# Capped attention and two expert layers on one core: a q load on another queue, a v copy on another engine, a 64-column transpose and a last tile copied in two halves

## The chip, the core and the metric

The program runs on one core of one Trainium2 chip. The metric is the device time of one execution in microseconds (us), the median of several runs. The engines named below are PE (TensorE, matrix products), DVE (VectorE), ACT (ScalarE), POOL (GpSimd) and SP (SyncE, which only issues transfers here). Each engine takes its instructions in order; ACT and SP also issue DMA transfers, in order with the rest of their work.

## The reference, cut to what matters

```python
scores = q @ k^T / sqrt(64)               # 2 batches x 12 heads, 448 x 64 each
scores = cap * tanh(scores / cap)         # cap = 30
attn = exp(scores - max);  attn /= sum(attn)
x = (attn @ v), heads side by side        # 896 tokens x 768
h = x @ w_in1;   g = elu(h);     x = g @ w_out1     # 768 -> 2048 -> 768
h = x @ w_in2;   g = relu(h)**2; out = g @ w_out2   # the same sizes
```

Inputs and output are float32 in HBM; the four weight matrices arrive as float64 words.

## The kernel before, in words

**Precision.** Every float32 operand x of a product is split into a high part (rounded to the PE's float32r format) and a low part (x minus the high part). A product of two operands is three PE products: high by high, high by low, low by high. So each operand costs a copy (the high part) and a subtraction (the low part) on some engine.

**Attention.** The 24 heads are worked on in 12 pairs (`n` from 0 to 11); two pairs make a group `g` whose k, q and v come with the same loads. A head has 448 rows: three full blocks of 128 and a last one of 64. `load_group` (L103) issues the loads. `what` says which: "k" loads three blocks of k and its last rows (into `kz`, where the rest is zero, two transfers, L127), "q" loads three blocks of q (L118) and its last 64 rows (into `qz`, L122), "v" three blocks of v (L133), "w" its last rows (`vs`, L139). All go out on SP's queue except the first pair's q, the cap and the first weights, which go out on ACT's.

For each pair, `turn` (L170) has the PE transpose four blocks of k and four of q into the tile `pt` in PSUM (L168; there is one such tile), `high` (L186, ACT) and `low` (L192, DVE) split them. `scores` (L235, PE) makes a fourth of the scores into one of two `sc` tiles, `tanh` (L244, ACT) and `exp` (L252, ACT) follow, `split_p` (L263 copy, L264 subtraction, both DVE) splits the result into `ph` and `pl`, and `pv` (L287, PE) multiplies by v, whose parts `vh` and `vl` were made by `prep_v` (L153 copy on POOL for pairs 0 and 1 and on DVE from pair 2 on; L154 subtraction on POOL). `pv_out` (L296, ACT) copies the sums out; `norm` and `norm_x` (L309, L327 to L334, DVE, with three small transfers on SP's queue) divide by the row sums and split the result into `xh` and `xl`. The order of the work in the loop L574 is written by hand and overlaps four pairs: while pair n is at its tanh, pair n-1 is at its second half of `pv`, pair n+1 at its `high` and `low`, pair n+2 at its transposes. In iteration n the DVE's order is: second half of `split_p(n-1)`, `prep_v(n+1)`, `low(n+1)`, then `norm(n-2)`, `norm_x(n-3)`, first half of `split_p(n)`. In iterations 1 and 2 the DVE also makes one piece of weights (`second`, L607, L587).

Before the loop, `first_pair` (L198) turns and splits pair 0 in three pieces, with products of the identity matrix in between (L196, `idle_products`) whose results nobody reads. Its copies (L220, ACT) and subtractions (L222, DVE) are of 384, 512 and 128 columns. After it come the scores of pair 0 and `turn(1)`; `turn(2)` is issued in iteration 0 (L612), ahead of `pv(0, 0)`.

The issue order of the loads at the start, on SP's queue (L537 to L547): pair 0's k; pair 1's k and q; pair 0's v; the second group's k and q (L544); pair 1's v; weights; the second group's v.

**Expert layers.** The weights stream in by pieces, are turned from float64 words into high and low parts on DVE and ACT, and four stages of products follow (L521 to L523, then L745 to L747 for the last). The last stage writes the output by blocks of 128 tokens and 432, then 336 columns: `evac_out` (L730) copies one PSUM accumulator to a tile `o`, on DVE for even token blocks and on ACT for odd ones (L732), and SP issues the store (L733). The last of these is token block 6, alone in its group (L758).

The lines that set this order:

```python
load_group(1, "kq")                                        # L544
(nc.vector if n > 1 else nc.gpsimd).tensor_copy(h, vn)     # L153, in prep_v(n)
nc.tensor.transpose(to, src, ident)                        # L168, in turn_one
(nc.scalar.copy if t % 2 else nc.vector.tensor_copy)(o, acc)   # L732
```

Of the kernel before, what the change touches and what calls it, by code (L numbers as in the profile page):

```python
# [26 lines left out]
def attention_moe_kernel(  # L27
# [12 lines left out]
    nc = tc.nc  # L40
    B, H, S, D = q.shape
    NT, DM = out.shape
    DFF = w_in1.shape[1]
    P = 128
    NFULL = S // P
# [10 lines left out]
    ident = const.tile([P, P], F32, name="ident")  # L56
# [24 lines left out]
    W = 512  # L81
# [18 lines left out]
        if i < 2:  # L100
            eng.memset(vss[i][:, :, D:], 1.0)

    def load_group(g, what="kqvw", pp=None, dma=nc.sync.dma_start):  # L103

        if 2 * g >= len(pairs):
            return
        b, hp = pairs[2 * g]
        h0, nh = (0, 4) if pp is None else (2 * pp, 2)
        hs = slice(2 * hp + h0, 2 * hp + h0 + nh)
        if g not in nat:  # L110
            nat[g] = {x: lp.tile([P, NFULL, 4, D], F32, name=x, tag=x) for x in "kqv"}
        tail = slice(NFULL * P, S)
        for x, src in (("k", k), ("q", q)):
            if x in what:
                t = nat[g][x][:, :, h0:h0 + nh]
                src = src[b, hs]
                for c in range(NFULL):
                    dma(  # L118
                        t[:, c], src[:, c * P:(c + 1) * P].rearrange("h p d -> p h d")
                    )  # L120
                if x == "q":
                    dma(  # L122
                        qzs[g % 2][:D, h0:h0 + nh], src[:, tail].rearrange("h p d -> p h d")
                    )
                else:
                    for hh, r in enumerate(ROWS):
                        dma(  # L127
                            kzs[g % 2][r, h0 // 2:(h0 + nh) // 2, r],
                            src[hh::2, tail].rearrange("h p d -> p h d"),
                        )  # L130
        if "v" in what:
            for c in range(NFULL):
                dma(  # L133
                    nat[g]["v"][:, c, h0:h0 + nh],
                    v[b, hs, c * P:(c + 1) * P].rearrange("h p d -> p h d"),
                )
        if "w" in what:
            for hh, r in enumerate(ROWS):
                dma(  # L139
                    vss[g % 2][r, h0 // 2:(h0 + nh) // 2, :D],  # L140
                    v[b, hs][hh::2, tail].rearrange("h p d -> p h d"),
                )

    def prep_v(n):
        if n >= len(pairs):
            return
        g, pp = divmod(n, 2)
        vh, vl = vhs[n % 3], vls[n % 3]
        vn = nat[g]["v"][:, :, 2 * pp:2 * pp + 2]
        h, l = (t.rearrange("p (c h) d -> p c h d", h=2)[:, :, :, :D] for t in (vh, vl))  # L150


        (nc.vector if n > 1 else nc.gpsimd).tensor_copy(h, vn)  # L153
        nc.gpsimd.tensor_tensor(l, vn, h.bitcast(F32), op=ALU.subtract)  # L154


# [2 lines left out]
    def turn_one(to, n, u, c):  # L159
        g, pp = divmod(n, 2)  # L160
        hs = slice(2 * pp, 2 * pp + 2)
        if c < NFULL:
            src = nat[g]["kq"[u]][:, c, hs].rearrange("p h d -> p (h d)")
        elif u == 0:
            src = kzs[g % 2][:, pp]
        else:
            src = qzs[g % 2][:, hs].rearrange("p h d -> p (h d)")
        nc.tensor.transpose(to, src, ident)  # L168

    def turn(n):  # L170
        if n >= len(pairs):
# [26 lines left out]
    def first_pair():  # L198

        idle = psc.tile([P, 2, W], F32, name="sc", tag="sc")
        warm = lambda n: idle_products(idle, n)
        qk = [ap_.tile([P, 2, W], F32R, name=x, tag=x) for x in ("kqh", "kql")]
        st["qk", 0] = qk
        warm(8)
        pieces = []
        for u, cs, pool, tag, after in (
            (0, range(NFULL), ps1, "pt", 2),
            (1, range(NFULL + 1), ps1, "po", 0),  # L210
            (0, range(NFULL, NFULL + 1), psc, "sc", 6),
        ):
            t = pool.tile([P, 2, W], F32, name=tag, tag=tag)
            at = slice(cs[0] * P, (cs[-1] + 1) * P)
            for c in cs:
                turn_one(t[:, u, c * P:(c + 1) * P], 0, u, c)
            warm(after)
            pieces.append((t[:, u, at], *(x[:, u, at] for x in qk)))
        for t, h, l in pieces:
            nc.scalar.copy(h, t)  # L220
        for t, h, l in pieces:
            nc.vector.tensor_tensor(l, t, h.bitcast(F32), op=ALU.subtract)  # L222
# [115 lines left out]
    N0, N1 = 432, 336  # L338
# [196 lines left out]
    with tc.manual_schedule():  # L535
        fill_kq(0, nc.vector)
        load_group(0, "k", 0)  # L537
        load_group(0, "q", 0, dma=nc.scalar.dma_start)
        nc.scalar.dma_start(capt, cap.unsqueeze(0).to_broadcast([P, 1]))
        ws.load(nc.scalar.dma_start)  # L540
        load_group(0, "kq", 1)
        load_group(0, "vw", 0)
        fill_kq(1, nc.gpsimd)
        load_group(1, "kq")  # L544
        load_group(0, "vw", 1)
        ws.load()
        load_group(1, "vw")  # L547
# [2 lines left out]
        fill_v(2, nc.gpsimd)  # L550
        np_ = len(pairs)
        first_pair()
        nc.vector.reciprocal(tsc, capt)
        nc.vector.tensor_scalar(tsc, tsc, 1.0 / math.sqrt(D), None, op0=ALU.mult)
        prep_v(0)
# [18 lines left out]
        for n in range(np_):  # L574
            last = n == np_ - 1
            tanh(n, 0)
            if n:
                high(n + 1)
            tanh(n, 1)
            if not n:  # L580
                high(n + 1)
            split_p(n - 1, 1)
            prep_v(n + 1)
            exp(n, 0)
            low(n + 1)
            if n == 2:
                emit(second[3:])  # L587
            scores(n, 2)
            pv(n - 1, 1)
            scores(n, 3)  # L590
            if n:
                turn(n + 2)
            else:
                idle_products(ps1.tile([P, 2, W], F32, name="po", tag="po"), 9)
            norm(n - 2)
            if last:
                emit(ws.start())
            tanh(n, 2)
            pv_out(n - 1)
            if 2 <= n < 7:  # L600
                ws.load()
            tanh(n, 3)
            exp(n, 1)
            emit(norm_x(n - 3))
            split_p(n, 0)
            if n == 1:
                second = ws.whole()  # L607
                emit(second[:3])
            scores(n + 1, 0)
            scores(n + 1, 1)  # L610
            if not n:
                turn(2)  # L612
            if last:

                begun.append(new_acc())
                mm_in(0, 0, begun[0], xh, xl, kb[0:6:2])
            pv(n, 0)

            if n % 2:
                load_group((n + 3) // 2, "qv" if n > 1 else "v")  # L620
            else:
                load_group(n // 2 + 2, "k" if n else "kq")
                load_group(n // 2 + 1, "w" if n else "")


# [101 lines left out]
                todo = parts_of(acc[:, :, :S], yh, yl, m)  # L727
            return todo

        def evac_out(t, acc, c0, n):  # L730
            o = ep.tile([P, N0], F32, name="o", tag="e")[:, :n]
            (nc.scalar.copy if t % 2 else nc.vector.tensor_copy)(o, acc)  # L732
            nc.sync.dma_start(out[t * P:(t + 1) * P, c0:c0 + n], o)  # L733

        def moe2_out(todo, gh, gl):
            nt = NT // P

            def banks(n, width):
                tiles = [new_acc() for _ in range((n + 1) // 2)]
                return [tiles[i // 2][:, i % 2, :width] for i in range(n)]  # L740

            def mm(acc, f, t, w):
                gs = slice(t * P, (t + 1) * P)
                a, z = f == 0, f == FC - 1
                nc.tensor.matmul(acc, gh[:, f, gs], w[0], start=a, stop=False)  # L745
                nc.tensor.matmul(acc, gh[:, f, gs], w[1], start=False, stop=False)  # L746
                nc.tensor.matmul(acc, gl[:, f, gs], w[0], start=False, stop=z)  # L747

            acc = banks(nt, N0)
            for f in range(FC):  # L750
                w = ws.get((3, f))
                for t in range(nt):
                    mm(acc[t], f, t, w)
                emit(todo + ws.advance() + ws.advance())
                todo = []
            for t in range(nt):
                evac_out(t, acc[t], 0, N0)
            groups = [[0, 1], [2, 3], [4, 5], [6]]  # L758
            for ts in groups:
                acc = banks(len(ts), N1)  # L760
                for f in range(FC):
                    w = chunk(late["w"], f)
                    for a, t in zip(acc, ts):
                        mm(a, f, t, w)
                for a, t in zip(acc, ts):
                    evac_out(t, a, N0, N1)

        gh = gp.tile([P, FC, NT], F32R, name="gh", tag="gh")
        gl = gp.tile([P, FC, NT], F32R, name="gl", tag="gl")
# [45 lines left out]
```

## Time and profile before

| | us |
|---|---|
| median of 3 runs (595.73 to 596.18) | 595.95 |
| the profiled execution, whole | 594.1 |
| its span, first to last instruction | 592.3 |
| PE busy, of the span | 583.4 (98%) |
| DVE busy | 425.0 (72%) |
| ACT busy | 334.2 (56%) |
| POOL busy | 32.1 (5%) |

The profile is of one execution, taken by the hardware. An engine's rows give start and duration of its instructions and, in square brackets, how long the engine was idle before and what released it. Times inside the span count from its first instruction. "PEclk" is the granted clock of the PE as a share of full speed; rows show 1.00 (2.4 GHz) and 0.50 (1.2 GHz). "DMA share" is the mean busy share of the core's 16 DMA engines. The time between the span and the whole execution is 594.1 - 592.3 = 1.8 us. Durations overlap by a little where an engine begins an instruction before the last one is through.

### The profile page before, as it was taken

The page shows a single profiled execution, that of the slowest core. Times are in us where ns is not written, and L with a number is a line of the kernel's source. Part 1 is how long each engine was busy: PE and PEld are TensorE (multiplying, and loading weights), DVE is VectorE, ACT ScalarE, POOL GpSimd, SP SyncE. Part 2 cuts the span into 40 slices and gives each one's busy share as a digit, 9 for nine tenths or more (in the row PEclk, how much of TensorE's full clock was granted, in tenths as well). Part 3 has the DMA queues.
Part 4 walks back from the last instruction along what each step waited for, and adds up shares of the span by engine and source line. Part 5 has one row for each costly group of instructions (what it writes and reads, how often), then busy time and mean ns, then how long its engine had stood idle before and what let it go on. Part 6 is the DMA issues. An engine that isn't in the chain of part 4 may idle for free.

```text
span 592.3 us, 8596 instructions
## 1 busy us (share of the span) xinstructions
PE 583.4 (98%) x3062; PEld 528.0 (89%) x3062; DVE 425.0 (72%) x845; ACT 334.2 (56%) x484; POOL 32.1 (5%) x46
## 2 busy tenths in 40 slices
PE   8899999999999999999999999999999999999997
PEld 8677777788999999999999999999999999999997
DVE  4599999989999888665666657777777599981000
ACT  5699999827898777433333335666666645441000
POOL 3110110000000000000000000000000011230000
PEclk9899999999999999999999999999999999999999
DMA  5645651024444333233333344333333346622000
GB/s 128 158 103 140 161 148 42 33 75 144 135 133 134 106 98 100 76 128 106 116 98 107 111 132 132 107 107 107 108 114 113 108 136 184 184 70 106 24 23 37
DMA packets 81980, 64.76 MB, mean 109 GB/s; under 512 B 38416, under 2 KB 77072, under 8 KB 81936
## 3 DMA queue, kind: packets, MB, share of 16 engines
q1 hardware_dynamic: 80432, 63.58, 36.8%
q10 hardware_dynamic: 1504, 0.62, 0.4%
q8 instruction: 24, 0.39, 0.3%
q14 instruction: 20, 0.16, 0.1%
HBM read 61.34 MB, written 2.80 MB: 108 GB/s over the span
## 4 chain that ended last, share of the span: by engine, by line
PE 90%; DMA 3%; DVE 3%; SPq 2%; ACT 1%; issue 1%; POOL 0%; ACTq 0%; POOLq 0%; DVEq 0%
PE acc L522 19%; PE acc L523 19%; PE acc L521 19%; PE po L287 8%; PE acc L746 7%; PE acc L745 7%; PE acc L747 7%; PE sc L235 4%; PE pt L168 1%; DMA q<-in_q_dram 1%; SPq L118 1%; DVE xn L327 1%; DMA far<-rd 1%; DMA bc<-far 1%; DMA qz<-in_q_dram 0%
## 5 line engine op out<-in xcount | busy, mean ns | idle before, releaser
L521 PE MATMUL acc<-xh,wh 128*128 128x448 f32 x384 | 139.8, 364 | 1.2 <-ACT xh L333 1.2
L522 PE MATMUL acc<-xl,wh 128*128 128x448 f32 x384 | 140.0, 365 | 0.2 <-DVE xl L334 0.2
L523 PE MATMUL acc<-xh,wl 128*128 128x448 f32 x384 | 139.9, 364 | 0.0
L446 ACT CAST wh<-wf 128x384 fp32r<-128x384 f32 (+2 forms) x114 | 57.9, 508 | 107.2 <-PE acc L522 87.5
L391 ACT ACTIVATE wf<-wst 128x384 f32<-128x384 f32 (+2 forms) x130 | 70.5, 543 | 60.5 <-DVE wl L441 33.7
L441 DVE TENSOR_TENSOR wl<-wf,wh 128x384 fp32r<-128x384 f32 (+2 forms) x116 | 63.6, 548 | 55.9 <-ACT wh L446 55.8
L521 PEld LDWEIGHTS acc<-xh,wh 128*128 128x128 f32 x384 | 72.1, 188 | 7.1 <-ACT xh L333 1.5
L522 PEld LDWEIGHTS acc<-xl,wh 128*128 128x128 f32 x384 | 72.1, 188 | 5.9 <-DVE xl L334 0.5
L523 PEld LDWEIGHTS acc<-xh,wl 128*128 128x128 f32 x384 | 72.1, 188 | 5.7 <-DVE wl L441 0.3
L432 DVE SCALAR_TENSOR_TENSOR wf<-wst,wf 128x384 uint32<-128x384 uint32 (+3 forms) x132 | 71.1, 539 | 0.1
L425 DVE SCALAR_TENSOR_TENSOR wf<-wst,wf 128x384 uint32<-128x384 uint32 (+3 forms) x132 | 70.9, 537 | 0.0
L522 PE MATMUL acc<-gl,wh 128*128 128x448 f32 x192 | 70.0, 365 | 0.0
L523 PE MATMUL acc<-gh,wl 128*128 128x448 f32 x192 | 70.0, 364 | 0.0
L521 PE MATMUL acc<-gh,wh 128*128 128x448 f32 x192 | 69.8, 364 | 0.0
L404 DVE TENSOR_SCALAR wf<-wf 128x384 uint32<-128x384 uint32 (+3 forms) x132 | 54.4, 412 | 0.7
L400 DVE TENSOR_SCALAR wf<-wf 128x384 f32<-128x384 f32 (+3 forms) x132 | 45.7, 346 | 7.5 <-ACT wf L391 7.5
L244 ACT ACTIVATE e<-sc,tsc 128x896 f32<-128x896 f32 (+1 forms) x48 | 43.4, 911 | 2.9 <-PE sc L235 2.9
L732 DVE COPY o<-acc 128x432 f32<-128x432 f32 (+1 forms) x8 | 4.5, 557 | 53.8 <-PE acc L747 45.7
L746 PE MATMUL acc<-wl,gh 128*128 128x432 f32 x112 | 40.3, 359 | 0.0
L745 PE MATMUL acc<-wh,gh 128*128 128x432 f32 x112 | 40.0, 357 | 0.0
L747 PE MATMUL acc<-wh,gl 128*128 128x432 f32 x112 | 39.9, 356 | 0.0
L252 ACT ACTIVATE e<-e,capt 128x1792 f32<-128x1792 f32 (+1 forms) x24 | 38.6, 1609 | 0.8
(94 smaller groups left out, 933.0 us busy)
## 6 DMA issues: line engine op xcount, KB each, us to landing
wst<-in_moe_w_in_dram SPq DMA_DIRECT2D x63, 384.0 KB, 3.2
wst<-in_moe_w_out_dram SPq DMA_DIRECT2D x24, 384.0 KB, 3.2
wst<-in_moe_w_out_dram SPq DMA_DIRECT2D x16, 432.0 KB, 3.2
wst<-in_moe_w_out_dram SPq DMA_DIRECT2D x16, 336.0 KB, 2.9
wst<-in_moe_w_out_dram SPq DMA_DIRECT2D x12, 256.0 KB, 2.7
bc<-far SPq DMA_DIRECT2D x12, 224.0 KB, 3.3
k<-in_k_dram SPq DMA_DIRECT2D x15, 128.0 KB, 3.7
q<-in_q_dram SPq DMA_DIRECT2D x15, 128.0 KB, 2.9
```

What stands on the lines that cost most here:

```text
L391: nc.scalar.activation(self.f[i], hi.bitcast(F32), AF.Abs)
L404: v.tensor_scalar(fb, fb, 3, 0x3FFFFFFF, op0=ALU.logical_shift_left, op1=ALU.bitwise_and)
L425: v.scalar_tensor_tensor(out=fb, in0=hi, scalar=0xC0000000, in1=fb, op0=ALU.bitwise_and, op1=ALU.bitwise_or,)
L432: v.scalar_tensor_tensor(out=fb, in0=lo, scalar=29, in1=fb, op0=ALU.logical_shift_right, op1=ALU.bitwise_or,)
L441: (v if dst is None else nc.gpsimd).tensor_tensor(wl, self.f[i], wh.bitcast(F32), op=ALU.subtract)
L446: (v.tensor_copy if self.alone else nc.scalar.copy)(wh, self.f[i])
L521: nc.tensor.matmul(acc, w[0], x[0], start=first, stop=False)
L522: nc.tensor.matmul(acc, w[0], x[1], start=False, stop=False)
L523: nc.tensor.matmul(acc, w[1], x[0], start=False, stop=last)
L745: nc.tensor.matmul(acc, gh[:, f, gs], w[0], start=a, stop=False)
L746: nc.tensor.matmul(acc, gh[:, f, gs], w[1], start=False, stop=False)
L747: nc.tensor.matmul(acc, gl[:, f, gs], w[0], start=False, stop=z)
```

## The change

Four edits:

1. The second group's q (three transfers of 128 KB) is no longer issued on SP's queue between that group's k and pair 1's v; it is issued on ACT's queue right after `first_pair`. The last rows of q get a letter of their own, "z", and stay on SP's queue.
2. `prep_v(2)` makes its copy on POOL, not on DVE (POOL for n up to 2).
3. The last block of q, which has 64 rows, is transposed at 64 rows and 64 columns, not at 128; in `first_pair` the copy and the subtraction of q cover 448 columns, not 512.
4. The last output tile (token block 6, columns 432 to 767) is copied in two halves of 168 columns: DVE copies the first and SP stores it, ACT copies the second and stores it from its own queue.

```diff
-    def load_group(g, what="kqvw", pp=None, dma=nc.sync.dma_start):
+    def load_group(g, what="kqzvw", pp=None, dma=nc.sync.dma_start):
...
-                if x == "q":
-                    dma(
-                        qzs[g % 2][:D, h0:h0 + nh], src[:, tail].rearrange("h p d -> p h d")
-                    )
-                else:
+                if x == "k":
                     for hh, r in enumerate(ROWS):
                         dma(
                             kzs[g % 2][r, h0 // 2:(h0 + nh) // 2, r],
                             src[hh::2, tail].rearrange("h p d -> p h d"),
                         )
+        if "z" in what:
+            dma(qzs[g % 2][:D, h0:h0 + nh], q[b, hs, tail].rearrange("h p d -> p h d"))
...
-        (nc.vector if n > 1 else nc.gpsimd).tensor_copy(h, vn)
+        (nc.vector if n > 2 else nc.gpsimd).tensor_copy(h, vn)
...
-        nc.tensor.transpose(to, src, ident)
+        if u and c == NFULL:
+            nc.tensor.transpose(to[:, :D], src[:D], ident[:D, :D])
+        else:
+            nc.tensor.transpose(to, src, ident)
...
-            at = slice(cs[0] * P, (cs[-1] + 1) * P)
+            at = slice(cs[0] * P, min((cs[-1] + 1) * P, (W, S)[u]))
...
-        load_group(0, "q", 0, dma=nc.scalar.dma_start)
+        load_group(0, "qz", 0, dma=nc.scalar.dma_start)
...
-        load_group(0, "kq", 1)
+        load_group(0, "kqz", 1)
         load_group(0, "vw", 0)
         fill_kq(1, nc.gpsimd)
-        load_group(1, "kq")
+        load_group(1, "kz")
...
         first_pair()
+        load_group(1, "q", dma=nc.scalar.dma_start)
...
-                load_group((n + 3) // 2, "qv" if n > 1 else "v")
+                load_group((n + 3) // 2, "qzv" if n > 1 else "v")
             else:
-                load_group(n // 2 + 2, "k" if n else "kq")
+                load_group(n // 2 + 2, "k" if n else "kqz")
...
-        def evac_out(t, acc, c0, n):
+        def evac_out(t, acc, c0, n, parts=1):
             o = ep.tile([P, N0], F32, name="o", tag="e")[:, :n]
+            if parts == 2:
+                for i, (copy, dma) in enumerate((
+                    (nc.vector.tensor_copy, nc.sync.dma_start),
+                    (nc.scalar.copy, nc.scalar.dma_start),
+                )):
+                    h = slice(i * n // 2, (i + 1) * n // 2)
+                    copy(o[:, h], acc[:, h])
+                    dma(out[t * P:(t + 1) * P, c0 + h.start:c0 + h.stop], o[:, h])
+                return
...
-                    evac_out(t, a, N0, N1)
+                    evac_out(t, a, N0, N1, 2 if t == nt - 1 else 1)
```

## Rows read from the trace of the kernel before

**Rows 1.** The page, part 1: busy us (share of the span) and instructions.

```profile
PE 583.4 (98%) x3062; PEld 528.0 (89%) x3062; DVE 425.0 (72%) x845; ACT 334.2 (56%) x484; POOL 32.1 (5%) x46
```

**Rows 2.** The chain that ended last, in order of time: start us, us, what.

```profile
17.06 2.67 DMA qz<-in_q_dram
...
20.17 4.06 PE po L287 x12
...
30.18 2.67 PE po L287 x12
...
62.49 0.89 PE pt L168 x8
...
80.91 1.42 PE sc L235 x12
...
89.45 1.42 PE sc L235 x12
...
134.00 0.57 ACT xh L333
```

**Rows 3.** Busy us (instructions) of PE, PEld, DVE, ACT, POOL by stretch, PEclk, DMA.

```profile
15.00:20.00 5.00, 3.38 (x21) 2.11 (x21) 3.90 (x4) 2.85 (x4) 0.00 (x0) 1.00 0.61 136
20.00:25.00 5.00, 5.00 (x21) 4.25 (x22) 0.00 (x0) 3.66 (x3) 1.51 (x2) 0.66 0.67 172
26.00:130.00 104.00, 103.21 (x583) 79.17 (x583) 100.63 (x143) 88.55 (x91) 10.12 (x10) 1.00 0.40 101
```

**Rows 4.** Timeline, DVE: start us, us, engine, line, tiles, count [idle before].

```profile
26.01 0.55 DVE L153 CAST vh<-v 128x384 fp32r<-128x384 f32 x1 [7.04 <-DMA v<-in_v_dram]
...
27.54 1.08 DVE L263 CAST ph<-e 128x1792 fp32r<-128x1792 f32 x1
...
31.73 0.62 DVE L263 CAST ph<-e 128x896 fp32r<-128x896 f32 x1
...
40.23 0.62 DVE L263 CAST ph<-e 128x896 fp32r<-128x896 f32 x1
...
109.52 0.62 DVE L263 CAST ph<-e 128x896 fp32r<-128x896 f32 x1
```

**Rows 5.** Timeline, SP's queue, 13 to 24 us.

```profile
15.32 1.69 SPq L118 DMA_DIRECT2D q<-in_q_dram  x3
...
21.18 1.58 SPq L133 DMA_DIRECT2D v<-in_v_dram  x3
```

**Rows 6.** Timeline, ACT and its queue (ACTq), 0 to 38 us.

```profile
0.73 1.55 ACTq L118 DMA_DIRECT2D q<-in_q_dram  x3
...
9.67 1.91 ACT L244 ACTIVATE e<-sc,tsc 128x896 f32<-128x896 f32 x2 [1.72 <-PE sc L235]
...
20.21 0.96 ACT L186 CAST kqh<-pt 128x960 fp32r<-128x960 f32 x1 [2.32 <-PE pt L168]
...
22.11 1.79 ACT L252 ACTIVATE e<-e,capt 128x1792 f32<-128x1792 f32 x1
...
28.71 1.43 ACT L252 ACTIVATE e<-e,capt 128x1344 f32<-128x1344 f32 x1
...
37.34 1.42 ACT L252 ACTIVATE e<-e,capt 128x1344 f32<-128x1344 f32 x1
```

**Rows 7.** Timeline, POOL, 20 to 24 us.

```profile
21.50 0.50 POOL L153 CAST vh<-v 128x384 fp32r<-128x384 f32 x1 [7.32 <-DMA v<-in_v_dram]
22.08 1.01 POOL L154 TENSOR_TENSOR vl<-v,vh 128x384 fp32r<-128x384 f32 x1
```

**Rows 8.** Timeline, the copies of output tiles on DVE and ACT, from 540 us.

```profile
543.87 0.61 DVE L732 COPY o<-acc 128x432 f32<-128x432 f32 x1 [3.90 <-DMA out_dram<-o]
...
581.61 0.51 DVE L732 COPY o<-acc 128x336 f32<-128x336 f32 x1 [14.37 <-PE acc L747]
...
582.20 0.44 ACT L732 COPY o<-acc 128x336 f32<-128x336 f32 x1 [14.44 <-DVE o L732]
...
589.03 0.51 DVE L732 COPY o<-acc 128x336 f32<-128x336 f32 x1 [6.91 <-PE acc L747]
```

More of the change, by code (lines that the diff above doesn't have):

```diff
@@ L113, in load_group @@
         for x, src in (("k", k), ("q", q)):
+            src = src[b, hs]
             if x in what:
                 t = nat[g][x][:, :, h0:h0 + nh]
-                src = src[b, hs]
                 for c in range(NFULL):
```

## The prediction, made before the changed kernel ran

> **What bounds the kernel now.** I first read the busy shares: PE 98%, DVE 72% [rows 1]. That looks like a kernel with nothing to win beside the PE, but the shares are averages over stages, so next I read the stretches [rows 3]. From 26 to 130 us, the body of attention, DVE is busy 100.6 of 104 us and PE 103.2: two engines without slack. In the five microseconds from 15 PE works 3.38 only, and in the next five its mean clock is 0.66. DVE does nothing at all from 20 to 25 us. So the start of attention is the one loose stretch, and the DVE is the one to ask about.
>
> The timeline of DVE shows the idle time in one piece, 7.04 us, ended by a transfer of v [rows 4]. The instruction that waits is the copy for pair 2's v (L153), which pair 2's products need much later; but DVE takes its work in order, so `low(2)` and the split of pair 1's probabilities, from 27.54 on, queue behind it. From there DVE has no gap worth the name up to 130 us.
>
> The chain of waits shows what holds the PE [rows 2]. Around 17 to 20 us its turn(2) waits for the second group's q, and last for qz, issued at 17.06 and landed 2.67 later. SP issues in order, and the three q transfers before qz hold the queue for 1.69 us from 15.32 [rows 5]. Then pv(0,0), 12 products, takes 4.06 us where the same 12 of pair 1 take 2.67 [rows 2]: in that stretch the mean granted clock is 0.66, 2.4 GHz falling to 1.2 after the PE was fed poorly [rows 3]. Behind the loop comes the hand-over at 134 us, where PE waits for xh [rows 2]; that is at the end of a line of DVE work and transfers which starts from the last pv.
>
> **Edit 1, q to ACT's queue.** Removed from SP: three issues, so qz and everything behind it (pair 1's v, weights, the second group's v, the next groups' loads) goes out 17.06 - 15.32 = 1.74 us earlier [rows 2, 5]. qz lands at 15.32 + 2.67 = 18.0 and its transpose is done about 1.75 us earlier. Added on ACT: three issues, 1.55 us by those of pair 0's q, of half the size [rows 6], or 1.69 by SP's of the same size [rows 5]. They fit in the 1.72 us for which ACT waits before the first tanh [rows 6]; if they ran over by up to half a microsecond, ACT's idle 2.32 before high(2) would still cover most of it, since only 1.75 of that goes. Cost: nothing. q itself is issued by about 9.6 and has until 17.4 to land. Its traffic now runs beside pair 0's v and the second k; a k late by some tenths would take them from the gain, and that stays in the range.
>
> So high(2) moves from 20.21 to about 18.45, and with it tanh(1,1) and exp(1,0), whose end moves from 22.11 + 1.79 = 23.90 to 22.15 [rows 6]. For the PE there is the clock too: if it stays at 2.4 GHz through pv(0,0), 4.06 - 2.67 = 1.39 us are saved [rows 2], at worst nothing. I take it in full, since the poorly fed stretch shrinks by half. PE and what hangs on it then stand 1.75 + 1.39 = 3.1 us earlier.
>
> **Edit 2, the copy to POOL.** POOL makes such a copy in 0.50 us and the subtraction in 1.01 [rows 7], with 5% of its time used [rows 1]. v lands when DVE's copy starts today, 26.0, less 1.74 = 24.3; vl(2) is ready at 25.9, some ten microseconds before pv(2,0). Cost there: nothing. What DVE wins: it no longer waits for v. low(2) runs at 19.4, and the split of pair 1 (27.54 today) starts when exp(1,0) ends, 22.15: 5.4 us earlier. The work between 27.54 and 31.73 takes 4.19, so DVE comes to the second half of that split at 26.35; that half needs exp(1,1), which ends today at 28.71 + 1.43 = 30.14 and then at 27.0. So 27.0 for 31.73: DVE stands 4.7 us earlier [rows 4, 6]. The next place like it: exp(2,1) ends at 38.76 and DVE takes it up at 40.23, a slack of 1.47 [rows 4, 6]; DVE needs 4.7 - 3.1 = 1.6 of it and waits 0.1. That leaves 4.6.
>
> Is it kept? DVE runs from pair 2 to pair 10 at (109.52 - 40.23) / 8 = 8.66 us a pair [rows 4]; an undisturbed pair of the PE takes 89.45 - 80.91 = 8.54 [rows 2]. So PE, 1.5 us less far ahead, makes up 0.12 a pair over nine pairs, 1.1, and stands at 4.2 at the end of the loop, plus what edit 3 gives. I take 4.5 for the shift of the hand-over, between 4.2 and 4.6. The expert layers behind it are PE from end to end (136 us on), and come earlier by the same.
>
> The Trainium skill's page "SBUF — State Buffer", section "Who interferes with whom", says that GpSimd shares a port pair with VectorE by an exclusive lock, so a VectorE copy in a two-port mode or an operation with two SBUF inputs and a GpSimd operation block one another in full. That rule speaks against edit 2, and by it the sum would lose what rival B below gives.
>
> **Edit 3, 64 columns.** Eight transposes take 0.89 us, 0.11 each [rows 2]; half of one is 0.05 at best, ten times in the loop 0.5, at worst nothing. In a loop that goes by DVE it adds nothing; it only helps the PE to catch up, as above. Worth 0. The narrower copy in first_pair ends before qz lands: 0.
>
> **Edit 4, the last tile in halves.** DVE takes 0.61 for 432 columns and 0.51 for 336 [rows 8], so 0.335 for 168; ACT by the same share 0.44 x 0.335 / 0.51 = 0.29. Would both copy at once? In the pair at 581.61, DVE and ACT copy two banks of one PSUM tile, and ACT starts at 582.20, 0.08 after DVE's end, although the profile names nothing else that it waited for [rows 8]. If the halves follow one another in that way, the second ends at 589.03 + 0.335 + 0.08 + 0.29 = 589.74, today's copy at 589.54: 0.2 later. Side by side it would be 0.17 earlier. A slower issue on ACT's queue (0.52 by rows 6) adds up to 0.2. I take +0.2, with ends of -0.2 and +0.4.
>
> The skill's page "PSUM — Partial Sum Buffer", section "PSUM bank collisions raise a hardware error", says that two engines must not read one bank at once; the halves lie in one bank, so by it they have to follow one another, as the row shows for two banks of one tile.
>
> **The sum.** -4.5 + 0.2 = -4.3 us. The profiled execution took 594.1, with 1.8 us around its span of 592.3, and would take 589.8; the median of the runs stands 1.85 higher at 595.95, and I carry that over: 591.65, say 591.6.
>
> **Rivals.** A, the clock still falls. PE is better fed but still waits for kz and qz. Then PE stands 1.75 earlier only, exp(1,1) ends at 28.4, DVE at 3.3 earlier, and with the slack of 1.47 at the next place at 3.2: -3.1 + 0.2, 593.0.
>
> B, POOL and DVE in one another's way. POOL's two operations, 1.5 us from 24.3 on, come beside the subtraction of pair 1's split. If they hold DVE up for all of it, 0.65 is hidden (26.35 to 27.0) and 0.85 is lost: 592.5. In today's rows POOL's subtraction takes 1.01 with DVE idle [rows 3, 7]; no row has it beside that work.
>
> C, no change. The start moves but the loop's end doesn't, because some transfer behind the row sums sets it: 596.1 with the tail. Against it: DVE waits 3.4 us in 104 [rows 3].
>
> D, slower. If DVE does not move (the second half of split at 31.73 stays), PE, 3 to 4 us ahead, only comes earlier to its wait for xh at 134 us; that wait grows past 4 us, and the clock falls there as it did at 20 us, which cost 1.39. With the tail, 597.5. It decides at that one split: moved by less than about a microsecond, D holds.
>
> **How the numbers follow.** Forecast 0.62, A 0.18, B 0.08, C 0.06, D 0.06. The range runs from the forecast with both good ends (DVE 5.4 or transposes on top, tail -0.2: 590.3) to A with the bad tail and a tenth or two more (593.5). A measurement here can tell 0.2% from no change, 1.2 us; the forecast, A and B are beyond it: faster 0.88, same 0.06, slower 0.06.
>
> **What would show it.** Right: high(2) near 18.4; no clock of 0.5 from 20 to 24; DVE's split of pair 1 near 22; everything at the hand-over near 4.5 earlier; in the tail ACT's half behind DVE's. Wrong: a new idle stretch on DVE before 27, POOL rows longer than 0.5 and 1.0, or a longer PE wait at the hand-over.

## The result, and the profile after

The changed kernel is **slower**: 598.69 us median of 4 runs (598.31 to 599.73) against 595.84 (595.70 to 596.18) of the kernel before on the same chip, 2.85 us more, ratio 1.0056, 95% interval 1.0041 to 1.0070. Forecast were 591.6 us and a range from 590.3 to 593.5; slower had been given 0.06.

The profiled execution took 599.73 us, its span 597.9: 5.6 more than the span of before. The pair is an unlucky one: the other three runs of the changed kernel had spans of 596.5 to 597.1, and a second profiled execution of the kernel before, in the last experiment, had 593.4. So the rows below show the mechanism; its size is that of the medians.

ACT and its queue, 0 to 24 us, of the kernel after; this answers to [rows 6]:

```profile
6.83 0.27 ACT L221 CAST kqh<-sc 128x128 fp32r<-128x128 f32 x1
13.71 3.79 ACTq L118 DMA_DIRECT2D q<-in_q_dram  x3
17.60 1.91 ACT L245 ACTIVATE e<-sc,tsc 128x896 f32<-128x896 f32 x2 [10.50 <-DMA kz<-in_k_dram]
20.24 1.81 ACT L253 ACTIVATE e<-e,capt 128x1792 f32<-128x1792 f32 x1
```

ACT ends the last copy of `first_pair` at 7.1 us and does nothing until 17.6. The three issues do not follow one another: the first goes out at 13.71, the last at 17.10. The first tanh starts at 17.60, where it started at 9.67, and the releaser named is a transfer which tanh doesn't read: the last rows of k of the second group. The chain of waits, in order of time, leads to the same place:

```profile
14.52 2.56 DMA kz<-in_k_dram
17.08 0.02 issue
17.10 0.39 ACTq L118
...
17.60 1.02 ACT e L245
18.62 0.04 issue
18.66 2.90 PE sc L236 x8
```

The third q transfer is issued 0.02 us after kz has landed. Why q waits for kz can't be seen in a profile; the program's own list of instructions has it. It gives each transfer of SP's and ACT's queues one of eight semaphores, DMAHW0 to DMAHW7, by turns and for both queues together, and a transfer waits until the one which had its semaphore before has landed. On ACT's queue:

```
9 L118 DMA q_138<-in_q_dram 128x4x64 [waits DMAHW0_49]
10 L118 DMA q_138<-in_q_dram 128x4x64 [waits DMAHW2_49]
11 L118 DMA q_138<-in_q_dram 128x4x64 [waits DMAHW5_49]
```

By SP's part of that list DMAHW0 belongs to the second `vs` transfer of pair 0, DMAHW2 to the second block of k of group 1, and DMAHW5 to the second `kz`: transfers which SP issues between 11 and 15 us (the chain above has the last of them). In the kernel before, q's transfers wait for such turns too, but on SP, which has nothing else to do. On ACT the tanh, `high` and exp of two pairs stand behind them.

The stretches of the kernel after; columns as in [rows 3]:

```profile
10.00:15.00 5.00, 0.96 (x6) 0.44 (x4) 1.21 (x3) 0.00 (x0) 1.50 (x2) 0.99 0.53 119
15.00:20.00 5.00, 1.34 (x6) 0.83 (x6) 0.00 (x0) 2.40 (x3) 0.48 (x1) 0.50 0.73 164
20.00:25.00 5.00, 5.00 (x23) 4.79 (x21) 4.04 (x3) 4.89 (x5) 1.04 (x2) 0.50 0.80 194
```

PE works 2.3 us of the ten from 10 on, and its granted clock falls to 0.50 (1.2 GHz) from 15 to 25 us, longer than before. DVE and POOL, answering to [rows 4, 7]:

```profile
28.87 1.16 DVE L193 TENSOR_TENSOR kql<-pt,kqh 128x960 fp32r<-128x960 f32 x1 [1.98 <-ACT kqh L187]
33.15 1.09 DVE L264 CAST ph<-e 128x1792 fp32r<-128x1792 f32 x1 [3.12 <-PE po L288]
...
37.35 0.62 DVE L264 CAST ph<-e 128x896 fp32r<-128x896 f32 x1
```

```profile
25.99 1.27 POOL L151 CAST vh<-v 128x384 fp32r<-128x384 f32 x1 [4.87 <-DMA v<-in_v_dram]
27.34 1.00 POOL L152 TENSOR_TENSOR vl<-v,vh 128x384 fp32r<-128x384 f32 x1
```

The split of pair 1 starts at 33.15, not 27.54: 5.61 later, of the 7.93 by which the tanh is late. And a new wait stands before it. `low(2)` is done at 30.0 and v is no longer asked for, but the copy into `ph` waits 3.12 us for PE. From here on nothing changes: the second half of that split is 5.62 later, the copy of xh at the hand-over (139.62 for 134.00) 5.62, the span 5.6. The end, answering to [rows 8]:

```profile
594.63 0.33 DVE L741 COPY o<-acc 128x168 f32<-128x168 f32 x1 [6.91 <-PE acc L759]
594.99 0.33 SPq L742 DMA_DIRECT2D out_dram<-o  x1
595.00 0.30 ACT L741 COPY o<-acc 128x168 f32<-128x168 f32 x1 [6.76 <-DVE o L741]
595.33 0.36 ACTq L742 DMA_DIRECT2D out_dram<-o  x1
```

ACT's half starts when DVE's has ended. From the start of the first copy to the end of the span there are 597.9 - 594.63 = 3.27 us, and in the kernel before 592.3 - 589.03 = 3.27.

### The profile page after: what moved, and what is told of

The parts are those of the page before. It is cut to its first block, busy times and chain, and to the rows that moved or that the text cites. A ratio compares the mean times of both kernels' runs of the same rounds, so it can differ in the third digit from the quotient of the medians.

```text
span 597.9 us, 8598 instructions
## 1 busy us (share of the span) xinstructions
PE 582.8 (97%) x3062; PEld 528.8 (88%) x3062; DVE 424.4 (71%) x844; ACT 334.6 (56%) x485; POOL 33.4 (6%) x47
## 4 chain that ended last, share of the span: by engine, by line
PE 90%; DMA 3%; DVE 3%; SPq 1%; ACT 1%; issue 1%; POOL 0%; ACTq 0%; POOLq 0%; DVEq 0%
PE acc L523 19%; PE acc L524 19%; PE acc L522 19%; PE po L288 7%; PE acc L758 7%; PE acc L757 7%; PE acc L759 7%; PE sc L236 4%; PE pt L169 1%; DMA q<-in_q_dram 1%; DVE xn L328 1%; PE po L197 1%; ACT e L245 1%; DMA far<-rd 1%; DMA bc<-far 1%
## 5 line engine op out<-in xcount | busy, mean ns | idle before, releaser
L245 ACT ACTIVATE e<-sc,tsc 128x896 f32<-128x896 f32 (+1 forms) x48 | 43.3, 910 | 11.7 <-DMA kz<-in_k_dram 10.5
L522 PEld LDWEIGHTS acc<-gh,wh 128*128 128x128 f32 x192 | 36.1, 188 | 2.9
```

Source lines behind the costliest of these rows:

```text
L522: nc.tensor.matmul(acc, w[0], x[0], start=first, stop=False)
```

## The experiments

Unless it says otherwise, each is the changed kernel with the edit shown. Ratios are to the kernel before, timed beside it.

**1. q back on SP's queue.** Edits 2 to 4 stay.

```diff
-        load_group(1, "kz")
+        load_group(1, "kqz")
...
-        load_group(1, "q", dma=nc.scalar.dma_start)
```

> The changed kernel with edit 1 undone: the second group's q is issued on SP's queue again, edits 2 to 4 stay. Theory W (each q transfer on ACT's queue waits until an earlier transfer, whose completion semaphore it takes over, has landed, and ACT stands still with it): the first tanh is back near 9.5 us instead of 17.6; low(2) no longer waits for v, DVE begins the split of pair 1 at 23.9 instead of 27.54, and its second half at 30.1 instead of 31.7; gain over the kernel before about 1.5, less 0.2 for the tail: 594.5 (593.5 to 595.5). Rival P (the copy on POOL is what costs): it stays slower than before, 597 to 599. Rival T (the tail in halves costs): slower than before by the whole 2.8.

Measured: 595.63 us, ratio 1.0001 (0.9983 to 1.0018). The tanh is back at 9.98, so the loss is gone, but the gain which edit 2 was to bring isn't there. Its DVE timeline says why:

```profile
21.29 1.16 DVE L193 TENSOR_TENSOR kql<-pt,kqh 128x960 fp32r<-128x960 f32 x1 [2.01 <-ACT kqh L187]
27.14 1.61 DVE L264 CAST ph<-e 128x1792 fp32r<-128x1792 f32 x1 [4.69 <-PE po L288]
```

The 7 us of waiting for v [rows 4] have become 4.69 of waiting for PE, and the split starts at 27.14 for 27.54. There is one `ph` tile; pv(0,1) reads pair 0's from it, and pair 1's can't be written before that. The copy also takes 1.61 us, not 1.08, with POOL's subtraction beside it until 27.79, and the second half of the split starts at 31.85, 0.12 later than before.

**2. Three tiny transfers in q's place.** q stays on SP; ACT issues three transfers of 512 bytes where the change issues q.

```diff
-        load_group(1, "q", dma=nc.scalar.dma_start)
+        junk = const.tile([P, 3], F32, name="junk")
+        for i in range(3):
+            nc.scalar.dma_start(junk[:, i:i + 1], cap.unsqueeze(0).to_broadcast([P, 1]))
```

> As the first kernel (q on SP's queue), but three transfers of 512 bytes each stand on ACT's queue where the changed kernel has q; what they load is used by nobody. Theory W: size does not matter, ACT stands still until the three earlier transfers have landed, the first tanh begins between 15 and 17 us, and the time is near that of the changed kernel, 597 to 599. Rival C (three transfers of 128 KB on a second queue collide with SP's and are slow to issue): tiny ones cost 1.5 us of issue at most, hidden in ACT's gap before the first tanh, so the time is that of the first kernel, about 594.5.

Measured: 601.18 us, ratio 1.0097 (1.0072 to 1.0122). ACT and its queue:

```profile
7.29 0.27 ACT L221 CAST kqh<-sc 128x128 fp32r<-128x128 f32 x1
13.38 3.32 ACTq L556 DMA_DIRECT2D junk<-in_cap_dram  x3
16.81 1.90 ACT L245 ACTIVATE e<-sc,tsc 128x896 f32<-128x896 f32 x2 [9.25 <-DMA junk<-in_cap_dram]
```

1.5 KB in the place of 384 KB hold ACT up for 9.25 us, nearly the 10.50 of q. For that wait it matters little what is moved, and how much; that ACT issues it there does. The time is another matter: 601.18 is above the 597 to 599 expected and 2.5 above the changed kernel. The profiled execution, at 599.13 the shortest of six, doesn't show why, and that stays open.

**3. q on ACT's queue, but early**, right behind the first weights, with `first_pair` still to come.

```diff
         ws.load(nc.scalar.dma_start)
+        load_group(1, "q", dma=nc.scalar.dma_start)
...
         first_pair()
-        load_group(1, "q", dma=nc.scalar.dma_start)
```

> The changed kernel, but q's three transfers on ACT's queue are issued right behind the first weights, ahead of first_pair. Theory W: the transfers whose semaphores they take over have landed by about 6 to 8 us, ACT is held by a microsecond or two at its first copies at most, q lands long before 17 us, and the gain that was forecast comes, less what 384 KB cost the loads of pair 1: 591.6 to 593.5. Rival N (nothing to win at the start, the hand-over or the transfers behind the row sums set the end): within 1 us of the kernel before. Rival C: slower than before, since the same transfers run beside more of SP's.

Measured: 592.82 us, ratio 0.9956 (0.9941 to 0.9971). Faster than both kernels. The three issues now wait for transfers of the first microseconds; ACT, DVE, POOL and the stretches:

```profile
4.83 2.42 ACTq L118 DMA_DIRECT2D q<-in_q_dram  x3
...
10.94 1.91 ACT L245 ACTIVATE e<-sc,tsc 128x896 f32<-128x896 f32 x2 [1.29 <-PE sc L236]
...
19.56 0.96 ACT L187 CAST kqh<-pt 128x960 fp32r<-128x960 f32 x1 [0.41 <-PE pt L167]
```

```profile
24.83 1.09 DVE L264 CAST ph<-e 128x1792 fp32r<-128x1792 f32 x1 [3.12 <-PE po L288]
26.03 2.14 DVE L265 TENSOR_TENSOR pl<-e,ph 128x1792 fp32r<-128x1792 f32 x1
28.09 1.18 DVE L388 TENSOR_SCALAR wf<-wst 128x384 uint32<-128x384 uint32 x1
...
29.97 0.62 DVE L264 CAST ph<-e 128x896 fp32r<-128x896 f32 x1
```

```profile
25.32 0.97 POOL L151 CAST vh<-v 128x384 fp32r<-128x384 f32 x1 [3.08 <-DMA v<-in_v_dram]
26.36 2.68 POOL L152 TENSOR_TENSOR vl<-v,vh 128x384 fp32r<-128x384 f32 x1
```

```profile
15.00:20.00 5.00, 4.74 (x33) 3.43 (x33) 4.51 (x4) 4.56 (x6) 0.31 (x1) 1.00 0.52 115
20.00:25.00 5.00, 5.00 (x28) 3.81 (x27) 1.56 (x3) 4.12 (x4) 1.52 (x2) 1.00 0.73 181
```

PE is fed (4.74 of 5 us for 3.38), the clock stays at 1.00 through 20 to 25 us where it was 0.66 [rows 3], and pv(0,0)'s 12 products, 4.06 us in [rows 2], take 2.63 from 19.53 on in the chain of waits. Still the split starts only 2.7 earlier than before, behind the same wait for PE. And once it runs, POOL stands beside it: copy and subtraction take 0.97 and 2.68 for 0.50 and 1.01 [rows 7], and DVE's L388, otherwise 0.35, takes 1.18. The ends fit one after the other: DVE's subtraction ends at 28.17, POOL's, begun at 26.36, at 29.04, that is 0.87 behind it, and L388 at 29.27, 0.23 behind that.

**4. No q on ACT, another order on SP**: the second group's k, q and last rows ahead of pair 0's v.

```diff
-        load_group(0, "vw", 0)
         fill_kq(1, nc.gpsimd)
-        load_group(1, "kz")
+        load_group(1, "kqz")
+        load_group(0, "vw", 0)
...
-        load_group(1, "q", dma=nc.scalar.dma_start)
```

> The changed kernel, but q is back on SP's queue and the second group's k, q and last q rows are issued ahead of pair 0's v. Nothing is added to ACT's queue. Theory W with the forecast's mechanism: qz is issued about 2.8 us earlier than before and lands near 17, PE's clock stays at 1.00 from 20 to 25 us, DVE begins the split of pair 1 near 22; v of pair 0 lands late, near 17, and takes back some: 592 to 593.5. Rival N: within 1 us of the kernel before.

Measured: 594.65 us, ratio 0.9991 (0.9973 to 1.0010): no difference that can be told. turn(2) is done at 17.6 and the clock stays at 1.00, but now PE's pv(0,0) waits 1.60 us for POOL's copy of pair 0's v, the transfer that was overtaken. The split starts at 24.88, not near 22, after 5.09 us of waiting for PE; its second half is 1.64 earlier than before, but that is gone at the hand-over (see "Is it kept?" below).

**5. Edit 1 alone**, edits 2 to 4 undone.

> The kernel before with edit 1 alone. Theory W: the whole loss is in this edit; ACT is held until about 17.5 us as in the changed kernel, DVE takes the split of pair 1 when pv(0,1) ends, near 33; the time is that of the changed kernel within 1 us, 2.5 to 4 us above the kernel before. Rival M (edits 2 to 4 hide part of a larger loss): more than 1 us slower than the changed kernel.

Measured: 598.73 us, ratio 1.0048 (1.0029 to 1.0067), not told apart from the 1.0056 of the whole change. The profile is of an execution of 2020.5 us, so no rows are read from it. The loss lies in edit 1, and in the presence of that loss the other three edits together are worth nothing that can be measured.

**6. q on POOL's queue**, at its old place in the order, where no wait is asked of it.

```diff
+        load_group(1, "q", dma=nc.gpsimd.dma_start)
...
-        load_group(1, "q", dma=nc.scalar.dma_start)
```

> The changed kernel, but the three transfers of q are issued on GpSimd's queue, in the order of the code behind the second group's k and kz, where they wait for no earlier transfer. Theory W: nothing is held on ACT, the first tanh begins near 9.6, qz lands near 18, pv(0,0) runs at the full clock, DVE takes the split of pair 1 when pv(0,1) ends, near 24; 2.5 to 4 us faster than the kernel before. Rival C (384 KB so early collide with the loads of pair 1): turn(1) waits, the first tanhs or high(1) move back by 1 us or more, and the gain is under 2.

Measured: 593.73 us, ratio 0.9973 (0.9955 to 0.9991), a gain short of the 2.5 us expected. The tanh is at 10.28, the clock 1.00, and the split starts at 24.72. The rows beside it are like those of experiment 3: POOL's copy keeps its 0.50, but its subtraction takes 2.68 from 26.25 on, and DVE's L388 1.17.

**7. Experiment 3 without edit 2**: pair 2's v copied on DVE again (`n > 1` in L151).

> As the third kernel (q early on ACT's queue), with edit 2 undone: pair 2's v is copied by DVE again. Theory L (in the third kernel POOL's copy and subtraction stood beside DVE's work and held it: 1.18 us for a 0.35 us operation, 0.95 us lost in all; against that DVE did not wait for v): DVE waits for v until about 25, the split of pair 1 starts near 26.5, no DVE row is longer than before; 0.5 to 1.5 us slower than the third kernel. Rival (edit 2 is worth nothing, since the split waits for pv(0,1) anyway): equal to it within 0.4.

Measured: 594.27 us, ratio 0.9981 (0.9965 to 0.9997), 1.45 slower than experiment 3. DVE waits for v until 25.76 and starts the split at 27.29. So edit 2 is worth something, but only once q is early: then PE lets the split go at 24.83 (experiment 3), before v is there for DVE's copy. With q on SP (experiment 1) PE lets it go at 27.14 only.

**8. One of q's three blocks on ACT**, the other two on SP.

> The changed kernel with only one of q's three blocks on ACT's queue, the other two on SP's at their old place. Theory W: this one transfer waits for one earlier transfer only, the one that held the first of three in the changed kernel until 13.71; so ACT is free near 14.1, the first tanh begins near 14.2 instead of 17.6, and the time lies between the first kernel (q on SP's queue) and the changed one. Rival C: one issue costs 0.4 us, hidden; the time is that of the first kernel.

Measured: 596.02 us, ratio 1.0003 (0.9987 to 1.0020), not told apart from experiment 1. ACT waits for the first of the three semaphores only:

```profile
13.18 0.37 ACTq L118 DMA_DIRECT2D q<-in_q_dram  x1
13.66 1.91 ACT L245 ACTIVATE e<-sc,tsc 128x896 f32<-128x896 f32 x2 [5.21 <-DMA vs<-in_v_dram]
```

The releaser is `vs`, the owner of DMAHW0 by the list. The tanh is 3.9 us earlier than with three and 3.7 later than with none (9.98), and those 3.7 cost no time that can be told.

**9. Experiment 3, and on SP's queue the second group's v ahead of pair 1's last rows of v and of the weights.**

```diff
-        load_group(0, "vw", 1)
+        load_group(0, "v", 1)
+        load_group(1, "v")
+        load_group(0, "w", 1)
         ws.load()
-        load_group(1, "vw")
+        load_group(1, "w")
```

> The same as the version with the second group's q on ACT's queue right behind the first weights (592.8 us, 0.9956 of the kernel before), with one change: on SP's queue the second group's v goes out right behind pair 1's v, ahead of vs and of the weights. Theory (POOL's copy and subtraction for pair 2 hold up DVE's split of pair 1 when they stand beside it: there a copy of 0.50 took 0.97, DVE's subtraction L388 1.18 instead of 0.35, and the second half of the split came 0.95 later than its work alone asks for): v lands about 1.7 us earlier, POOL works while DVE still waits for pv(0,1), the long rows go back to 0.35 to 0.6, the second half of the split starts near 29.0 instead of 29.97, and the time is 591.9, between 0.5 and 1 us less. Rival (the lock costs the split some time, but what DVE reaches there is set by exp(1,1) or by PE anyway): rows get shorter, time equal within 0.3 us.

Measured: 592.09 us, ratio 0.9934 (0.9910 to 0.9958). POOL and DVE:

```profile
22.92 0.50 POOL L151 CAST vh<-v 128x384 fp32r<-128x384 f32 x1 [0.94 <-DMA v<-in_v_dram]
23.50 1.02 POOL L152 TENSOR_TENSOR vl<-v,vh 128x384 fp32r<-128x384 f32 x1
```

```profile
24.54 1.09 DVE L264 CAST ph<-e 128x1792 fp32r<-128x1792 f32 x1 [3.11 <-PE po L288]
25.73 2.03 DVE L265 TENSOR_TENSOR pl<-e,ph 128x1792 fp32r<-128x1792 f32 x1
27.67 0.35 DVE L388 TENSOR_SCALAR wf<-wst 128x384 uint32<-128x384 uint32 x1
...
28.74 0.62 DVE L264 CAST ph<-e 128x896 fp32r<-128x896 f32 x1
```

POOL is through before DVE's split begins; every row has its old length, and from the first to the second half of the split it is 4.20 again, after 5.14 in experiment 3. The second half comes 1.23 earlier and the span is 1.2 shorter (589.7 for 590.9). The medians say 0.7, the ratios 1.3, and the intervals overlap, so the gain over experiment 3 is shown in the rows and not by the times alone.

**10. Experiment 9, with `ph` and `pl` in two tiles each**, one for the first four blocks and one for the last two.

```diff
-                ap_.tile([P, NB - 1, S], F32R, name=x, tag=x, bufs=1) for x in ("ph", "pl")
+                [ap_.tile([P, m, S], F32R, name=x + str(j), tag=x + str(j), bufs=1) for x in ("ph", "pl")]
+                for j, m in enumerate((4, NB - 5))
```

> The version just named, and ph and pl are each two tiles, one for the first four blocks and one for the last two, of the same total size, so that the first half of split_p(1) waits only for pv(0,0) and no longer for pv(0,1). Theory (DVE's split of pair 1 waits for PE's last reading of the one ph tile): its first copy starts near 22 instead of 24.8, the second half then waits for exp(1,1) near 27, and the time is 590.5 to 591.5. Rival (PE is the bound by then, or the second half waits for exp(1,1) in both versions): the first copy starts earlier, the time stays within 0.3 us of the version before.

Measured: 592.07 us, ratio 0.9940 (0.9921 to 0.9959), equal to experiment 9: the rival's time, though not by either wait that it named. The wait for PE is gone and the copy starts at 23.26, but there it meets POOL again:

```profile
23.26 1.36 DVE L265 CAST ph<-e 128x1792 fp32r<-128x1792 f32 x1 [1.58 <-ACT e L253]
24.73 2.65 DVE L266 TENSOR_TENSOR pl<-e,ph 128x1792 fp32r<-128x1792 f32 x1
...
28.36 0.62 DVE L265 CAST ph<-e 128x896 fp32r<-128x896 f32 x1
```

The subtraction of 2.03 takes 2.65 (POOL's beside it 1.74), and of 1.28 us won at the first copy 0.38 are left at the second. DVE comes to the second half without a wait. The copy started later than the 22 expected, since exp(1,0) ends at 23.23.

**11. Experiment 1 with the same two tiles.**

> The changed kernel with q back on SP's queue (that alone ran at 595.6 us, no gain over the kernel before, although DVE no longer waits for v), and ph and pl each in two tiles. This takes the one tile's wait by itself: in the version with q on SP's queue DVE's split of pair 1 waited 4.69 us until 27.14 for PE's pv(0,1). Theory (the second edit won nothing because of that wait): the first copy starts near 24.4, when exp(1,0) is done, the second half waits for exp(1,1) near 30.2 instead of 31.3, and the time is 594.5, about 1.0 to 1.6 us less than with one tile. Rival (what the second half waits for is exp(1,1), which goes by PE and not by DVE): the first copy moves, the time stays at 595.6.

Measured: 594.98 us, ratio 0.9970 (0.9955 to 0.9985); experiment 1 had 1.0001.

```profile
24.87 1.09 DVE L265 CAST ph<-e 128x1792 fp32r<-128x1792 f32 x1 [1.57 <-ACT e L253]
...
31.23 0.63 DVE L265 CAST ph<-e 128x896 fp32r<-128x896 f32 x1 [1.09 <-ACT e L253]
```

The copy starts 2.27 earlier, so it was the one tile that held it. The second half then waits for exp(1,1) and wins 0.62 only (31.85 to 31.23); the hand-over comes 0.71 earlier. By medians the gain is 0.65 us, by ratios 1.8. Both the theory's wait and the rival's are there, one behind the other.

**12. The kernel before once more.**

> The kernel before once more, for its clock and its rows in a second profiled execution. Its first profiled execution took 594.1 us while the median is 595.8. If the granted clock over the whole span sets the spread between executions, an execution near 596 shows a mean clock some tenths of a per cent below 0.997 and the same times up to 130 us; if the start varies, the rows up to 30 us differ.

Measured: 595.19 us, span 593.4, mean clock 0.997 as in the first profile, though 1.1 us longer. Between these two the start varies, not the clock: the split of pair 1 is at 28.24 for 27.54, the hand-over at 135.05 for 134.00. But two are few. Over the 82 executions of this kernel that were timed beside the experiments, a lower mean clock goes with a longer time: 595.4 us on average at 0.997 (33 of them), 598.0 at 0.991 (7).

Where the time sits can be read from four starts and the span, in us:

| kernel | first tanh | split of pair 1 | its second half | xh, hand-over | span |
|---|---|---|---|---|---|
| before, first profile | 9.67 | 27.54 | 31.73 | 134.00 | 592.3 |
| before, second profile | 8.74 | 28.24 | 32.43 | 135.05 | 593.4 |
| after | 17.60 | 33.15 | 37.35 | 139.62 | 597.9 |
| experiment 1 | 9.98 | 27.14 | 31.85 | 135.21 | 593.5 |
| experiment 3 | 10.94 | 24.83 | 29.97 | 132.54 | 590.9 |
| experiment 4 | 9.13 | 24.88 | 30.09 | 134.18 | 592.5 |
| experiment 7 | 10.94 | 27.29 | 31.48 | 135.08 | 593.4 |
| experiment 9 | 10.70 | 24.54 | 28.74 | 131.42 | 589.7 |
| experiment 11 | 8.95 | 24.87 | 31.23 | 134.50 | 592.8 |

From the hand-over to the end it is 458.3 us in every line, to within 0.1. Whatever these executions win or lose, they do so before the hand-over.

## Why the prediction was wrong

**Edit 1, "They fit in the 1.72 us for which ACT waits before the first tanh ... Cost: nothing".** This is the step that failed. The three issues were priced at their own length, 1.55 to 1.69 us, and that was enough (0.37 to 0.39 each, 1.14 in all); what was left out is when each may go out. ACT stood still for 10.5 us in place of 1.7, since each transfer waits for an older transfer on SP's queue to land. Experiment 2 shows that the issue at this place is enough, experiment 8 that ACT waits for one semaphore with one issue, experiment 5 that the whole loss is here, and experiments 3 and 6 that q itself may leave SP without loss. The text took a transfer without a data dependence for one without a wait, and so never asked what is queued behind it on ACT. SP's issues of q stand back to back in [rows 5] and don't show that they wait for turns as well. But another place in the trace of before does show such a wait, in its chain:

```profile
1.79 2.72 DMA q<-in_q_dram
4.51 0.02 issue
4.53 0.37 SPq L118
```

The first line is the third block of pair 0's q, issued by ACT; the last is SP's issue of a block of pair 1's k, 0.02 us after that q has landed. The issue has no use for q. By the list of instructions of that kernel it waits for DMAHW4, which q had before. So the sign was there to be read: an issue on one queue that is released by a transfer of the other.

The Trainium skill's page "DMA: Bandwidth & Descriptors", section "Issuing engines are not separate DMA queues", says that issuing from several engines only saves sequencer time, which is usually small. The rows show what was saved here, 1.87 us for the issue of qz (15.19 for 17.06 on SP's queue), and add what there is to lose: 7.93 at the tanh.

**Edit 2, "the split of pair 1 (27.54 today) starts when exp(1,0) ends, 22.15".** The second failed step. It named the producer of the data and forgot the last reader of the tile that is written over. Experiment 1 measures it: 0.4 us earlier than in the kernel before where 5.4 had been forecast, and nothing at the second half. Experiment 11 takes that wait away, and the copy starts at 24.87, when exp(1,0) ends, as the step had it. With the early q of experiment 3 edit 2 is worth 1.45 us (experiment 7), not nothing.

**Rival B, POOL and DVE in one another's way,** was given 0.08 and priced at 0.85 us. It is real. Where POOL's two operations stand beside the split, in experiment 3, the split's second half comes 5.14 after the first instead of 4.20: 0.94 lost, and experiment 9 gets it back by moving the transfer. The Trainium skill's page "SBUF — State Buffer", section "Who interferes with whom", says of a VectorE instruction in a two-port mode that it contends with GpSimd, that whoever issues first has the shared ports for the whole instruction and that the other is blocked; an operation with two SBUF inputs contends as well. The rows of experiment 3 come near to that: POOL's subtraction ends 0.87 behind DVE's (by itself it takes 1.01), and L388 0.23 behind POOL's (by itself 0.35). In the changed kernel itself B costs DVE nothing at this place. POOL's copy takes 1.27 beside DVE's subtraction of pair 0, but that one keeps its 1.09 (25.80 to 26.89), and DVE then waits for ACT until 28.87. In experiment 1, where q is loaded as before, the copy of the split loses 0.53.

**The clock and the early q** were right as mechanisms, shown in experiment 3 and not in the change: no fall from 20 to 25 us, and 4.06 - 2.63 = 1.43 us less for pv(0,0), where 1.39 was forecast. In the change itself the starved stretch grew and the clock stayed at 0.50 through all of 15 to 25 us. Rival A had the sign of this and not the size. When the clock falls is not settled by how busy PE is over those five us: in experiment 4 PE works 3.11 of the five from 15 on, less than the 3.38 of before, and the clock stays at 1.00.

**"Is it kept?"** In part. In the change 5.62 later stays 5.62, and in experiment 3 the second half of the split is 1.76 earlier than in the first profile of before and the hand-over 1.46. But in experiment 4 1.64 earlier becomes 0.18 later, and in experiment 7 0.25 earlier becomes 1.08 later. The last wait before the hand-over, in the kernel before and in experiment 4:

```profile
132.72 1.25 DVE L327 TENSOR_TENSOR xn<-pvs,bc 64x448 f32<-64x448 f32 x2 [2.58 <-DMA bc<-far]
132.90 1.25 DVE L328 TENSOR_TENSOR xn<-pvs,bc 64x448 f32<-64x448 f32 x2 [3.24 <-DMA bc<-far]
```

`bc` is the last of the three small transfers behind the row sums. DVE waits for it 2.58, 3.24 and, in experiment 7, 3.87 us; why it lands later there isn't shown. That some transfer there sets the loop's end was rival C, given 0.06: not what made the change slower, but part of what a gain at the start loses on the way. Rival D, a gain lost at the hand-over, isn't what made it slower.

**Edit 3** at nothing: not tried alone. From one pair's transposes to the next an undisturbed PE takes 8.47 us in the change (85.63 to 94.10) and 8.54 before (79.88 to 88.42), 0.07 less where 0.05 at best was forecast; DVE sets the pace, 8.66 a pair in both, so the time doesn't show it. **Edit 4**: the halves follow one another, as read from [rows 8], but the cost was 0.0 and not +0.2. The last store goes out 0.70 us after the first copy began, for 0.54 before, and, of 84 KB and not 168, lands in 1.7 us and not 1.8; the ends agree to the tenth that these rows show.

## What to carry to other kernels

Before a transfer is moved to a compute engine's queue, look in the program's list of instructions for what its issue waits on: a semaphore that is shared by turns ties it to transfers of other queues, and everything behind it on that engine pays. A transfer whose place in the list lies behind early transfers waits little (experiment 3: first tanh at 10.94 for 9.67); the same transfer 18 places later in the list held the tanh until 17.60. And when a wait is taken away, ask of the next instruction not only who makes its input but who last reads its output tile, and which engine will now work beside it.

## What was not expected

Three transfers of 512 bytes held ACT nearly as long as three of 128 KB: 9.25 us for 10.50. And two profiled executions of one unchanged kernel differ by 0.70 us at 28 us and by 1.1 in the span, so a single pair of profiles shows where time goes, but not amounts below about a microsecond.
